# Sigmoid attention and two chained feed-forward layers in split float32: another order of the seven block products, and where the operands of the next pair are made

## The chip, the cores and the metric

The kernel runs on one core of a Trainium2 chip. The metric is the device time of one execution in microseconds (us), the median of several runs. Engines: PE (TensorE) multiplies, with PEld as its weight loads; DVE (VectorE), ACT (ScalarE) and POOL (GpSimd) work elementwise; SP (SyncE) issues nearly all DMAs. Each engine works through its own queue in order.

## The reference

```python
def _attn_ref(q, k, v):                      # 4 batches, 12 heads, 448 rows, 64 wide
    scores = (1 / np.sqrt(64)) * q @ k.transpose(0, 1, 3, 2) - np.log(448)
    return 1 / (1 + np.exp(-scores)) @ v

x = attention output as (1792, 768)
h = x @ moe_w_in                             # layer one: 768 -> 2048 -> 768
x = np.maximum(h, 0) ** 2 @ moe_w_out
h = x @ moe2_w_in                            # layer two, the same sizes
out = (np.maximum(h, 0) + alpha * np.minimum(h, 0)) @ moe2_w_out
```

Inputs q, k, v are float32; the weights and alpha come as float64.

## The kernel before

**Split operands.** A float32 operand of a product is kept as two float32r tiles, a high part (a cast by ACT) and the rest (a subtraction by DVE or POOL), and each product is three matmuls: high by high, high by rest, rest by high.

**Stages.** Attention comes first, twelve rounds `d` (L307), two blocks of two heads in each. Then 32 units (L510), numbered here 0 to 31: layer one with batches 0 and 1 ("pair" 0) is units 0 to 7, layer one with pair 1 units 8 to 15, layer two with pair 0 units 16 to 23, with pair 1 units 24 to 31. A unit takes 256 of the 2048 hidden columns, in two blocks `j` of 128, for the 896 tokens of its pair, in two halves `t` of 448.

**A unit.** First come seven block products of the Strassen-Winograd scheme instead of eight (`product(k)` L375, 9 matmuls each, into three PSUM banks `hb`). After each, `after(n, k)` (L403) adds the result to the running sums e21, e12, e22, e11 and, where one of the four hidden blocks is complete, `slopes` (L382) applies the layer's function and makes its high part, and `low` (L399) its rest, in `G`. In layer one `slopes` is three ACT instructions; in layer two it is two Relus on ACT, one DVE instruction that joins them with `nal` (alpha, negated), and an ACT cast. Then `out_products` (L448) multiplies `G` by the split output weights `WO`: 12 outputs of 448 columns in layer one, 14 of 384 in layer two, 6 matmuls each. Five PSUM banks `ob` take turns; the first four outputs begin with block j = 1 (two high matmuls each, then one of the rest each), and j = 0 follows. `collect` (L470) adds each bank to `acc` by one DVE instruction, or by an ACT copy in the first unit of a pair.

**Other work of a unit.** It is hung on the steps "i0" to "i6" (after each block product) and "o0" to "o13" (after each output) by `at` (L521). `out_parts` splits the output weights of this unit: ACT casts, POOL subtracts. For the next unit `weight_sum` makes four sums of blocks of its input weights on POOL, and `weight_parts` splits the seven blocks, 384 columns at a time (ACT, DVE). Weights are read once as float64 (`load` L82, two buffers `raw`), turned into float32 by two ACT instructions (`scale`) and a DVE one (`join`), and kept in DRAM; the second pair of each layer reads the kept words. So `scale` and `join` run in units 0 to 6 and 14 to 22.

**Change of pair.** The block products need seven split operands `X[0]` to `X[6]` of the pair's tokens. They are made (`x_jobs` L146: four sums and seven splits, three instructions of 448 columns for each sum and six for each split) for pair 0 of layer one in attention's last rounds and in unit 0, and for the other pairs within units 7, 15 and 23, the last units before each change of pair (L515 and L565 to L576).

## Time and profile before

| | us |
|---|---|
| median of 3 runs | 1239.09 (1238.93 to 1240.93) |
| the profiled execution | 1239.76 |
| its span, first to last instruction | 1238.0 |
| PE busy | 1111.8 (90%) |
| DVE busy | 766.4 (62%) |
| ACT busy | 624.7 (50%) |
| POOL busy | 422.3 (34%) |
| mean granted TensorE clock | 0.945 of full |

Busy time is that of the whole span. The stages differ: a stretch of the span is read from the windows, a wait from the timeline or from the list of waits, and the share of an engine over the whole span says nothing of one stage. The granted clock is the share of the 2.4 GHz clock that PE was given; it has two levels here, 1.0 and 0.5.

### The profile page before, as it was taken

The numbers are of one execution on the slowest core, as the hardware profiler recorded it, in microseconds if no ns is written. First come the engines' busy times: TensorE is split into PE (matmuls) and PEld (weight loads), VectorE is DVE, ScalarE is ACT, GpSimd is POOL, SyncE is SP. The second block draws the span as 40 slices with busy tenths as digits, with TensorE's granted clock in tenths as the row PEclk, the third lists the DMA queues.
The fourth block names the chain that finished last, engine by engine and source line by source line (L and its number), as shares of the span: only waits on it lengthen the run. The fifth ranks groups of instructions, "written<-read, shape, count | busy, mean of one in ns | idle before, by whom it ended". The sixth has DMA issues, their size and how long they took to land.

```text
span 1238.0 us, 14888 instructions
## 1 busy us (share of the span) xinstructions
PE 1111.8 (90%) x5607; PEld 953.7 (77%) x5607; DVE 766.4 (62%) x1121; ACT 624.7 (50%) x1055; POOL 422.3 (34%) x312
## 2 busy tenths in 40 slices
PE   6999989999998899999977888888896888898888
PEld 4555558888887788899966877888885777888877
DVE  3556854667777735565578467666678445555554
ACT  3567757666664464433455655555444543223332
POOL 0002352444344533333365223333343333332221
PEclk8999998999999999999989888888998989998899
DMA  5577703544442111111224433433422211111002
GB/s 119 122 184 194 199 1 130 177 153 153 154 153 89 38 52 64 52 65 51 77 77 153 152 116 115 138 109 136 154 77 73 93 52 41 50 39 51 26 26 90
DMA packets 108008, 123.67 MB, mean 100 GB/s; under 512 B 54048, under 2 KB 86560, under 8 KB 107936
## 3 DMA queue, kind: packets, MB, share of 16 engines
q1 hardware_dynamic: 105440, 121.47, 31.7%
q10 hardware_dynamic: 2496, 1.25, 0.4%
q8 instruction: 44, 0.72, 0.2%
q14 instruction: 28, 0.23, 0.1%
HBM read 92.02 MB, written 30.67 MB: 99 GB/s over the span
## 4 chain that ended last, share of the span: by engine, by line
PE 61%; DVE 18%; ACT 14%; issue 3%; DMA 2%; SPq 0%; POOL 0%; ACTq 0%; POOLq 0%; DVEq 0%
PE o L444 30%; PE h L380 19%; DVE c L396 5%; PE av L264 4%; PE sc L244 4%; DVE wi L139 3%; ACT pos L394 3%; ACT c L395 3%; DVE x L158 2%; DVE g L401 2%; ACT g L397 1%; ACT g L388 1%; ACT c L387 1%; ACT c L389 1%; ACT wi L138 1%
## 5 line engine op out<-in xcount | busy, mean ns | idle before, releaser
L380 PE MATMUL h<-x,wi 128*128 128x448 f32 x2016 | 426.1, 370 | 14.7 <-DVE c L415 10.9
L380 PEld LDWEIGHTS h<-x,wi 128*128 128x128 f32 x2016 | 380.3, 189 | 54.6 <-DVE c L415 8.2
L444 PE MATMUL o<-wo,g 128*128 128x384 f32 x1344 | 282.8, 372 | 74.8 <-DVE g L401 64.6
L444 PEld LDWEIGHTS o<-wo,g 128*128 128x128 f32 x1344 | 265.8, 213 | 91.9 <-DVE g L401 76.4
L530 POOL TENSOR_TENSOR wo<-wo,wo 128x768 fp32r<-128x768 f32 x64 | 129.6, 2045 | 451.2 <-ACT wo L529 451.2
L444 PE MATMUL o<-g,wo 128*128 128x448 f32 x1152 | 253.7, 378 | 22.7 <-DVE g L401 12.9
L444 PEld LDWEIGHTS o<-g,wo 128*128 128x128 f32 x1152 | 221.1, 194 | 53.1 <-DVE g L401 21.9
L481 DVE TENSOR_TENSOR acc<-o,acc 128x384 f32<-128x384 f32 (+1 forms) x364 | 208.1, 582 | 81.1 <-PE o L444 80.7
L139 DVE TENSOR_TENSOR wi<-wi,wi 128x384 fp32r<-128x384 f32 x96 | 95.9, 999 | 67.6 <-ACT wi L138 67.6
L401 POOL TENSOR_TENSOR g<-c,g 128x448 fp32r<-128x448 f32 x64 | 77.2, 1206 | 154.7 <-ACT g L397 103.2
L407 ACT ACTIVATE c<-h 128x448 f32<-128x448 f32 x32 | 17.3, 542 | 184.1 <-PE h L380 184.1
L396 DVE SCALAR_TENSOR_TENSOR c<-c,nal,pos 128x448 f32<-128x448 f32 x64 | 59.7, 933 | 72.0 <-ACT c L395 72.0
L246 ACT ACTIVATE a<-sc,bias 128x896 f32<-128x896 f32 x72 | 69.4, 1006 | 35.9 <-PE av L264 22.6
L139 DVE TENSOR_TENSOR wi<-s,wi 128x384 fp32r<-128x384 f32 x128 | 74.1, 579 | 13.5 <-ACT wi L138 13.4
L409 DVE TENSOR_TENSOR c<-h,c 128x448 f32<-128x448 f32 x32 | 20.0, 624 | 100.3 <-PE h L380 60.9
L158 POOL TENSOR_TENSOR x<-acc,x 128x448 fp32r<-128x448 f32 x32 | 44.8, 1406 | 102.6 <-ACT x L157 102.6
L127 POOL TENSOR_TENSOR s<-wi 128x384 f32<-128x384 f32 x32 | 40.5, 1267 | 89.6 <-DVE wi L113 89.6
L397 ACT ACTIVATE g<-c 128x448 fp32r<-128x448 f32 x64 | 37.0, 578 | 65.4 <-DVE c L396 65.4
L138 ACT ACTIVATE wi<-s 128x384 fp32r<-128x384 f32 x128 | 60.7, 513 | 0.0
L157 ACT ACTIVATE x<-acc 128x448 fp32r<-128x448 f32 x84 | 42.9, 565 | 33.2 <-DVE acc L152 31.4
L264 PE MATMUL av<-a,v 128*64 128x448 f32 x288 | 59.4, 548 | 0.0
L158 DVE TENSOR_TENSOR x<-acc,x 128x448 fp32r<-128x448 f32 x52 | 50.2, 999 | 12.3 <-ACT x L157 12.2
(164 smaller groups left out, 1116.0 us busy)
## 6 DMA issues: line engine op xcount, KB each, us to landing
v<-in_v_dram SPq DMA_DIRECT2D x24, 192.0 KB, 2.9
nat<-in_q_dram SPq DMA_DIRECT2D x22, 192.0 KB, 3.8
nat<-in_k_dram SPq DMA_DIRECT2D x20, 192.0 KB, 3.4
out_dram<-acc SPq DMA_DIRECT2D x14, 192.0 KB, 2.7
raw0i<-in_moe_w_in_dram SPq DMA_DIRECT2D x2, 768.0 KB, 5.8
raw0o<-in_moe_w_out_dram SPq DMA_DIRECT2D x2, 768.0 KB, 6.5
raw1i<-in_moe_w_in_dram SPq DMA_DIRECT2D x2, 768.0 KB, 5.3
raw1o<-in_moe_w_out_dram SPq DMA_DIRECT2D x2, 768.0 KB, 5.9
```

Source lines behind the costliest of these rows:

```text
L138: nc.scalar.activation(W[i][:, 0], w, AF.Copy)
L139: (eng or nc.vector).tensor_sub(W[i][:, 1], w, W[i][:, 0])
L158: jobs.append(lambda c=c: eng().tensor_sub(X[i][:, 1, c], x[c], X[i][:, 0, c]))
L244: nc.tensor.matmul(ps[:, h, :S], kt[rows, at:at + P], qt[rows, :S], start=(i == 0), stop=(i == 2))
L246: nc.scalar.activation(sig[u, j], ps[:, :, :S], AF.Sigmoid, bias=bias[:, :1], scale=SCALE)
L264: nc.tensor.matmul(avs[u][h * D:(h + 1) * D, :S], vals[u][:, h, j, :], a[:, h, :], start=(u % 2 == 0 and j == 0), stop=(u % 2 == 1 and j = ...
L380: nc.tensor.matmul(ps, W[k][:, wp, c * P:(c + 1) * P], X[k][:, xp, c], start=(k < 3 and c == 0 and i == 0), stop=(c == KH - 1 and i == 2), ...
L396: nc.vector.scalar_tensor_tensor(out=e, in0=e, scalar=nal[:, f:f + 1], in1=up, op0=ALU.mult, op1=ALU.add)
L401: eng.tensor_sub(gl, e, gh)
L444: nc.tensor.matmul(ps, *ops, start=(begin and i == 0), stop=(end and i == len(ways) - 1), skip_group_check=True)
L481: nc.vector.tensor_add(part, ps, part)
L530: nc.gpsimd.tensor_sub(WO[j][:, 1], words["o"][:, j], WO[j][:, 0])
```

## The change

- **Order of the block products.** `BANK` is now (0, 1, 2, 1, 2, 0, 1), and the hidden blocks come complete in the order e22, e12, e11, e21, one after each of products 3 to 6, where before it was e11, e22, e12, e21. The second part of a block (in layer two the DVE instruction and the cast) and its rest are issued one and two products later (`hidden`, `second`, `low`). All rests are made on DVE.
- **Input weights.** One tile `W` for all blocks; `weight_parts` splits 768 columns at a time in four pieces (s12 at i4, a1 at o0, a2 with 384 at o2, s34 at o3); the four sums run on DVE (i2, i3). The rests of the output weights stay on POOL, in four halves (i2 to i5).
- **Two banks at once.** `two` holds two PSUM tiles of two banks; a pair of outputs is added by one DVE instruction (768 or 896 columns). Seven of the eight banks are in use.
- **Words.** `turn_of`: scaling and joining now run in units 0 to 14, all in layer one; the words of layer two are joined in units 7 to 14 and go from `raw` straight to DRAM. `recall` reads kept words from unit 6 on.
- **X operands of the next pair.** X[0] to X[3] are made in units 1 to 6 of the pair before (four jobs a unit at o2 to o5: POOL sums and rests, ACT casts), through one tile `stage`, and sent to DRAM; the last unit of a pair loads them (i0 to i3) and makes X[4] to X[6] (DVE, DVE, POOL). Pair 1 of attention's output goes to DRAM (`late`) and comes back in unit 0. In attention all splits but X[6] are made, two subtractions of three on DVE (before one of three).

```diff
-        BANK = (0, 1, 2, 0, 1, 2, 1)
+        two = [psum.tile([P, 2, 512], F32, name="o0")]
...
+        BANK = (0, 1, 2, 1, 2, 0, 1)
+        OPERAND = (0, 4, 3, 5, 6, 1, 2)
...
+            for ways in (HIGH, LOW):
+                for os, both in pairs[:2]:
+                    for i in range(2):
+                        out_product(n, os[i], both[:, i], 1, ways, ways is HIGH, False)
+            for at, (os, both) in enumerate(pairs):
...
+                collect(n, os, both)
+                yield at
...
+        def wait_in_dram(p, i, c):
+            x_parts(p, i, c, nc.gpsimd, (stage[:, 0], stage[:, 1]))
+            nc.sync.dma_start(out=x_kept[i][:, :, c], in_=stage.bitcast(F32))
...
+            if V is not None:
+                if N > 1:
+                    at("i0", lambda: join(V, "i", 0))
+                    at("i1", lambda: join(V, "i", 1))
+                at("i0", lambda: load(V, "o", 0))
+                at("i1", lambda: load(V, "o", 1))
+                at("i5", lambda: scale(V, "o", 0, 1), lambda: scale(V, "o", 0, 0))
+                at("i6", lambda: join(V, "o", 0))
+                at("o0", lambda: scale(V, "o", 1, 1))
+                at("o1", lambda: scale(V, "o", 1, 0), lambda: join(V, "o", 1))
+            if U is not None:
+                at("i6", lambda: load(U, "i", 0))
+                at("o1", lambda: load(U, "i", 1))
+                at("o3", lambda: scale(U, "i", 0, 1), lambda: scale(U, "i", 0, 0))
+                at("o4", lambda: scale(U, "i", 1, 1))
+                at("o5", lambda: scale(U, "i", 1, 0))
...
+            step(3)
+            add(e22, 1, e22)
+            second22, low22 = hidden(n, e22, e22, 1, 1)
+            do("i3")
+            step(4)
+            add(e12, 2, e12)
+            second22()
+            second12, low12 = hidden(n, e12, e12, 0, 1)
+            do("i4")
+            step(5)
+            low22()
+            second12()
+            second11, low11 = hidden(n, hb[0][:, :S], e11, 0, 0)
+            do("i5")
+            step(6)
+            add(e21, 1, e21)
+            low12()
+            second11()
+            second21, low21 = hidden(n, e21, e21, 1, 0)
+            do("i6")
+            for i in out_products(n):
+                if i == 0:
+                    low11()
+                    second21()
+                if i == 1:
+                    low21()
+                do(f"o{i}")
```

DVE's queue from the middle of a layer-two unit into its outputs, before (c12 and so on are the sums e12 and so on, g0 and g1 the two tiles of `G`, o0 to o4 the output banks, wi the split input weights):

```order
L139 TENSOR_TENSOR wi3_79<-wi_87,wi3_79 128x384
L419 TENSOR_TENSOR c12_1765<-h2_1773,c12_1765 128x448
L396 SCALAR_TENSOR_TENSOR c12_1765<-c12_1765,nal_69,pos0_1767 128x448
L401 TENSOR_TENSOR g1_1762<-c22_1764,g1_1762 128x448
L423 TENSOR_TENSOR c21_1763<-h1_1772,c21_1763 128x448
L396 SCALAR_TENSOR_TENSOR c21_1763<-c21_1763,nal_69,pos1_1768 128x448
L401 TENSOR_TENSOR g0_1761<-c12_1765,g0_1761 128x448
L481 TENSOR_TENSOR acc1_75<-o4_1776,acc1_75 128x384
L139 TENSOR_TENSOR wi6_82<-wi_87,wi6_82 128x384
L481 TENSOR_TENSOR acc1_75<-o0_1769,acc1_75 128x384
L139 TENSOR_TENSOR wi1_77<-s2_84,wi1_77 128x384
```

and now (o0 and o1 are the tiles of two banks):

```order
L415 SCALAR_TENSOR_TENSOR c22_1787<-c22_1787,nal_69,pos0_1790 128x448
L137 TENSOR_TENSOR wi_77<-sums_78,wi_77 128x768
L417 TENSOR_TENSOR g1_1795<-c22_1787,g1_1795 128x448
L415 SCALAR_TENSOR_TENSOR c12_1788<-c12_1788,nal_69,pos1_1791 128x448
L582 TENSOR_TENSOR c21_1786<-h1_1800,c21_1786 128x448
L417 TENSOR_TENSOR g0_1794<-c12_1788,g0_1794 128x448
L415 SCALAR_TENSOR_TENSOR c11_1789<-c11_1789,nal_69,pos0_1790 128x448
L469 TENSOR_TENSOR acc1_1796<-o1_1802,acc1_1796 128x768
L417 TENSOR_TENSOR g0_1794<-c11_1789,g0_1794 128x448
L415 SCALAR_TENSOR_TENSOR c21_1786<-c21_1786,nal_69,pos1_1791 128x448
L137 TENSOR_TENSOR wi_77<-words_i_79,wi_77 128x768
L469 TENSOR_TENSOR acc1_1796<-o0_1798,acc1_1796 128x768
```

The split of s12 (`wi_77<-sums_78`) now stands ahead of the rest of e22, and between the first output's addition and the second's stand a rest, a layer-two join and the split of a1.

ACT's queue from the end of unit 9 (layer one, pair 1) into unit 10, before (L407 is the copy of the first product of unit 10):

```order
L389 ACTIVATE c21_1763<-c21_1763 128x448
L138 ACTIVATE wi6_82<-wi_87 128x384
L138 ACTIVATE wi1_77<-s2_84 128x384
L138 ACTIVATE wi2_78<-s1_83 128x384
L138 ACTIVATE wi4_80<-s3_85 128x384
L138 ACTIVATE wi5_81<-s4_86 128x384
L407 ACTIVATE c21_1763<-h0_1771 128x448
L529 ACTIVATE wo1_1760<-wo_88 128x768
L529 ACTIVATE wo0_1759<-wo_88 128x768
```

and now (raw words of layer two, `stage` the next pair's operands, L588 the copy of unit 10's first product):

```order
L136 ACTIVATE wi_77<-words_i_79 128x384
L158 ACTIVATE stage_1797<-acc0_76 128x448
L94 ACTIVATE raw19i0_3885<-raw19i0_3885 128x768
L96 ACTIVATE raw19i0_3885<-raw19i0_3885 128x768
L136 ACTIVATE wi_77<-sums_78 128x768
L158 ACTIVATE stage_1797<-acc0_76 128x448
L94 ACTIVATE raw19i1_3922<-raw19i1_3922 128x768
L158 ACTIVATE stage_1797<-acc0_76 128x448
L96 ACTIVATE raw19i1_3922<-raw19i1_3922 128x768
L588 ACTIVATE c21_1786<-h0_1799 128x448
L495 ACTIVATE wo1_1793<-words_o_80 128x768
```

Ahead of the copy stand now two casts into `stage` and the two scalings of a raw tile.

SP's queue from the end of unit 8 through unit 9, before (words of layer one that were kept):

```order
L88 DMA wi_87<-kept2i0_2027 128x768
L88 DMA wi_87<-kept2i1_2044 128x768
L88 DMA wo_88<-kept2o0_2158 128x768
L88 DMA wo_88<-kept2o1_2183 128x768
L88 DMA wi_87<-kept3i0_2246 128x768
L88 DMA wi_87<-kept3i1_2263 128x768
```

and now, from the middle of unit 9 into unit 10:

```order
L105 DMA kept18o0_3883<-raw18o0_3788 128x768
L86 DMA raw19i0_3885<-in_moe2_w_in_dram 128x6x128
L105 DMA kept18o1_3920<-raw18o1_3803 128x768
L86 DMA raw19i1_3922<-in_moe2_w_in_dram 128x6x128
L505 DMA kept_x8_0_3556<-stage_1797 256x1x448
L111 DMA words_i_79<-kept3i0_2249 128x768
L111 DMA words_i_79<-kept3i1_2264 128x768
L505 DMA kept_x8_0_3556<-stage_1797 256x1x448 x2
L105 DMA kept19i0_4009<-raw19i0_3885 128x768
L88 DMA raw19o0_4011<-in_moe2_w_out_dram 128x768
L105 DMA kept19i1_4024<-raw19i1_3922 128x768
```

Each load into `raw` stands behind the sending away of the words that lie in that buffer.

## Rows read from the trace of the kernel before

**Rows 1.** windows: us, busy us (count) by engine, PEclk, DMA share, GB/s
```profile
0.00:168.40 168.40, 157.74 (x1095) 86.84 (x1095) 95.19 (x117) 100.79 (x118) 22.45 (x22) 0.97 0.61 151
168.40:206.50 38.10, 31.33 (x137) 27.53 (x136) 23.13 (x27) 23.70 (x45) 18.34 (x13) 0.91 0.11 36
206.50:379.70 173.20, 169.09 (x812) 151.04 (x812) 121.55 (x179) 109.97 (x182) 70.22 (x49) 1.00 0.48 163
379.70:422.30 42.60, 32.70 (x136) 27.32 (x135) 34.42 (x45) 22.02 (x43) 23.67 (x18) 0.88 0.15 50
422.30:618.40 196.10, 194.74 (x947) 176.94 (x947) 106.71 (x174) 91.04 (x170) 74.16 (x58) 1.00 0.19 61
618.40:664.90 46.50, 34.09 (x136) 28.74 (x135) 39.64 (x50) 26.06 (x49) 25.01 (x18) 0.89 0.29 92
664.90:910.40 245.50, 215.57 (x1031) 200.36 (x1030) 161.14 (x241) 132.34 (x223) 83.56 (x58) 0.90 0.40 134
910.40:957.60 47.20, 34.09 (x148) 30.28 (x147) 37.79 (x53) 21.87 (x43) 25.03 (x18) 0.86 0.18 51
957.60:1204.00 246.40, 214.13 (x1031) 198.52 (x1030) 131.79 (x212) 88.17 (x168) 73.94 (x56) 0.92 0.15 50
```

**Rows 2.** timeline of PE in unit 28: start us, duration, instruction, count [idle before, releaser]
```profile
1098.17 13.17 PE L380 MATMUL h<-x,wi 128*128 128x448 f32 x63
1112.12 1.67 PE L444 MATMUL o<-wo,g 128*128 128x384 f32 x8 [0.78 <-ACT g L397]
1116.14 1.34 PE L444 MATMUL o<-wo,g 128*128 128x384 f32 x6 [2.34 <-DVE g L401]
1119.14 15.04 PE L444 MATMUL o<-wo,g 128*128 128x384 f32 x69 [1.67 <-DVE g L401]
```

**Rows 3.** timeline of DVE in unit 28
```profile
1112.99 0.62 DVE L419 TENSOR_TENSOR c<-h,c 128x448 f32<-128x448 f32 x1
1114.86 0.69 DVE L396 SCALAR_TENSOR_TENSOR c<-c,nal,pos 128x448 f32<-128x448 f32 x1 [1.25 <-ACT c L395]
1115.46 0.62 DVE L401 TENSOR_TENSOR g<-c,g 128x448 fp32r<-128x448 f32 x1
...
1119.87 0.56 DVE L481 TENSOR_TENSOR acc<-o,acc 128x384 f32<-128x384 f32 x1 [0.78 <-PE o L444]
1120.34 0.55 DVE L139 TENSOR_TENSOR wi<-wi,wi 128x384 fp32r<-128x384 f32 x1
```

**Rows 4.** timeline of ACT in unit 28
```profile
1115.58 0.58 ACT L397 ACTIVATE g<-c 128x448 fp32r<-128x448 f32 x1 [0.75 <-DVE c L396]
```

**Rows 5.** windows: a stretch of unit 28, and unit 31 with the final stores
```profile
1118.40:1125.20 6.80, 6.05 (x19) 6.06 (x20) 5.12 (x12) 2.64 (x6) 1.15 (x1) 0.50 0.20 59
1204.00:1238.00 34.00, 28.32 (x148) 26.17 (x147) 15.01 (x26) 8.73 (x15) 5.96 (x4) 1.00 0.26 82
```

**Rows 6.** timeline of PE in unit 31
```profile
1222.15 12.41 PE L444 MATMUL o<-wo,g 128*128 128x384 f32 x70 [1.68 <-DVE g L401]
```

**Rows 7.** groups by line: count, busy us, mean ns of one, idle before
```profile
L529 ACT ACTIVATE wo<-wo 128x768 fp32r<-128x768 f32 x64 | 50.4, 838 | 0.0
...
L158 POOL TENSOR_TENSOR x<-acc,x 128x448 fp32r<-128x448 f32 x32 | 44.8, 1406 | 102.6 <-ACT x L157 102.6
...
L217 DVE COPY flat<-tp 128x896 f32<-128x896 f32 x23 | 24.0, 1085 | 18.7 <-PE tp L214 18.7
```

**Rows 8.** DMA issues: count, KB each, median us from issue to landing
```profile
raw5i<-in_moe_w_in_dram SPq DMA_DIRECT2D x2, 768.0 KB, 5.4
...
kept5o<-wo SPq DMA_DIRECT2D x2, 384.0 KB, 3.4
```

**Rows 9.** timeline across the start of unit 4: PE and ACT
```profile
293.87 5.33 PE L380 MATMUL h<-x,wi 128*128 128x448 f32 x25
...
296.14 0.91 ACT L103 ACTIVATE raw5i<-raw5i 128x768 f32<-128x768 f32 x1 [1.82 <-DMA raw5i<-in_moe_w_in_dram]
...
297.75 0.53 ACT L407 ACTIVATE c<-h 128x448 f32<-128x448 f32 x1
```

More of the change, by code (lines that the diff above doesn't have):

```diff
@@ L107, in join @@
     def join(n, kind, j):
-        if (n, kind, j) not in raws:
-            return
         raw = raws.pop((n, kind, j))
-        to = words[kind][:, j]
-        nc.vector.scalar_tensor_tensor(out=to.bitcast(I32), in0=raw[:, :, 1], scalar=3, in1=raw[:, :, 0], op0=ALU.logical_shift_left, op1=ALU.bitwise_or)
-        _, f = source(n, kind, j)
-        keep = kept[UNITS[n][0], f, kind] = dpool.tile([P, DM], F32, name=f"kept{n}{kind}{j}")
-        nc.sync.dma_start(out=keep, in_=to)
-    def block(i, half):
-        return words["i"][:, i, half * HALF:(half + 1) * HALF]
@@ L121, in weight_sum @@
-    def weight_sum(i):
-        s1, s2, s3, s4 = sums
-        a11, a12, a21, a22 = block(0, 0), block(0, 1), block(1, 0), block(1, 1)
-        nc_ = nc.gpsimd
+        layer, p, fp = UNITS[n]
+        to = words[kind][:, j].bitcast(I32) if layer == 0 else raw.rearrange("p m t -> p (m t)")[:, :DM]
+        nc.vector.scalar_tensor_tensor(out=to, in0=raw[:, :, 1], scalar=3, in1=raw[:, :, 0], op0=ALU.logical_shift_left, op1=ALU.bitwise_or)
+        keep = kept[layer, 2 * fp + j, kind] = dpool.tile([P, DM], F32, name=f"kept{n}{kind}{j}")
@@ new lines, in join, with recall, turn_of, weight_sum @@
+        nc.sync.dma_start(out=keep, in_=to.bitcast(F32))
+    def recall(n, kind):
+        layer, p, fp = UNITS[n]
+        for j in range(2):
+            nc.sync.dma_start(out=words[kind][:, j], in_=kept[layer, 2 * fp + j, kind])
+    def turn_of(n):
+        return n if n < NB else n + NB
+    def weight_sum(i, eng=None):
+        (a11, a12), (a21, a22) = ([words["i"][:, j, h * HALF:(h + 1) * HALF] for h in range(2)] for j in range(2))
+        s = [sums[:, k * HALF:(k + 1) * HALF] for k in range(4)]
+        eng = eng or nc.vector
@@ L299, in fused_kernel @@
             early = [(0, "i", 0), (0, "i", 1), (0, "o", 0), (0, "o", 1), (1, "i", 0), (1, "i", 1)]
[L300 removed]
+            turns = [0]
             def either():
[L303 to L306 removed]
+                turns[0] += 1
+                return nc.gpsimd if turns[0] % 3 == 0 else nc.vector
+            ready_x = []
+            for what in X_ORDER[:-1]:
+                make = x_sums if what[0] == "s" else x_parts
+                ready_x += [lambda i=int(what[1]), c=c, make=make: make(0, i, c, either()) for c in range(KH)]
             for d in range(ND):
@@ L581, in fused_kernel @@
-            for i in range(7):
-                product(i)
-                after(n, i)
-                do(f"i{i}")
-                if i == 6:
-                    low(e21, 1, 0, nc.gpsimd)
-            for i in out_products(n):
+            if n == 0:
+                at("i0", lambda: nc.sync.dma_start(out=acc[1], in_=late))
+                for c in range(KH):
+                    at(f"i{c}", lambda c=c: x_parts(0, 6, c, nc.vector))
+            at("i0", lambda: out_parts(1), lambda: out_parts(0))
@@ new lines, in add, with step @@
+            def add(to, bank, other):
+                nc.vector.tensor_add(to, hb[bank][:, :S], other)
+            def step(k):
+                product(k)
+            step(0)
+            nc.scalar.activation(e21, hb[0][:, :S], AF.Copy)
+            do("i0")
+            step(1)
+            add(e12, 1, e21)
+            do("i1")
+            step(2)
+            add(e22, 2, e21)
+            do("i2")
+            step(3)
+            add(e22, 1, e22)
+            second22, low22 = hidden(n, e22, e22, 1, 1)
```

320 lines of the change are left out of this document (136 added, 184 removed).

## The prediction

> **What bounds the kernel now.** I read the windows by stage first, then the timelines of PE, DVE and ACT in single units, then the groups by line and the DMA issues. The windows [rows 1] show three regimes. Attention, the first 168.4 us, has PE busy for 157.7, and DVE for 95.2. Layer one's ordinary units (1 to 6, 8 to 14) are bound by PE at the full clock: 173.2 us for six units is 28.9 each, 196.1 for seven is 28.0. Layer two's (16 to 22, 24 to 30) take 245.5 and 246.4 us for seven, 35.1 and 35.2 each, at a granted clock of 0.90 and 0.92. The four units that make X operands, 0, 7, 15 and 23, take 38.1, 42.6, 46.5 and 47.2: there DVE is busy 23 to 40 us, POOL 18 to 25, and the clock is 0.86 to 0.91.
>
> Why layer two takes 7 us more than layer one, with as much to multiply, is seen in unit 28 [rows 2]: the seven products run through in 13.2 us, then PE waits 0.78, 2.34 and 1.67 us in the outputs, for the hidden blocks' parts. The 69 matmuls behind the last wait show 15.0 us, where 70 took 12.4 in unit 31, with a longest wait of 1.68 [rows 6]. The windows say why: unit 28 has 6.8 us at 0.50, half of 2.4 GHz, and unit 31 stays at 1.00 [rows 5]. So a layer-two unit is 13.0 + 84 x 0.177 = 27.9 us of work, 4.8 of waiting and 2 to 3.5 of half clock.
>
> DVE and ACT hand the blocks to and fro meanwhile [rows 3, 4]. The add of a product starts at 1112.99, the two Relus end 1.87 later, the join (0.69) and the rest (0.62) follow at 0.60 after each other, ACT's cast starts 0.04 after the join and takes 0.58.
>
> **The change, part by part.** Costs are against the profiled execution, 1239.8 us (1.8 of it outside the span of 1238.0); the median of the runs, 1239.1, is 0.7 lower.
>
> *Layer two's ordinary units, 13 of them (17 to 22, 25 to 30).* I walk DVE's new queue with T = 0 at the unit's first product. Product 4 can be added at 9.5 (five sevenths of 13.0, and 0.2). Add 0.55, join to 10.75, cast of e22 to 11.35, the Relus of e12 to 12.5. Then comes s12, 768 columns: ACT 0.84 [rows 7], to 13.3; DVE has no row of this size, two of 384 take 0.55 + 0.48 [rows 3], so 0.84 to 1.03, and I take 0.95: 14.25. Behind it in the same queue: the rest of e22, 14.8; join of e12, 15.45; its cast, 16.05; the Relus of e11, 17.0; its join, 17.7; cast and the Relus of e21, 19.5; its join, 20.2; cast, 20.8; then a1, 0.84 and 0.95, to 22.6; and only then the addition of the second pair of banks, 768 columns again, to 23.5. PE's side: outputs from 13.0, the eight high matmuls to 14.45, wait 0.4 for the rest of e22, 0.55 and 0.3 for e12's parts, the first two pairs done at 18.6, the first added by 18.75, third pair to 20.9. The fourth needs the second tile: it waits to 23.5, **2.6 us**. Four pairs of 12 x 0.177 follow: 32.1. That is 4.2 us of waiting against 4.8. Its longest wait is above the 2.34 that went with a half clock in unit 28 and above the 1.68 that did not in unit 31 [rows 2, 5, 6], so I keep the half clock at the price of [rows 1]: a clock of 0.92 over 246.4 us is 19.7 us for seven units, 2.8 each. 34.9 against 35.1: **-3** for 13 units. With the first units of the two pairs, 16 and 24, whose outputs ACT copies (-2), and unit 31, which has no s12 and no a1 (-2): **-7**.
>
> The double addition itself: one of 384 takes 0.56 and the next starts 0.48 later [rows 3], so two in one save some 0.1 us of DVE and release the first bank 0.4 later. DVE is busy 131.8 of 246.4 us in layer two's second half [rows 1], far from full, so I count the saving at nothing and the late release within the waits above. The Trainium skill (Perfetto Trace Analysis, Optimizing Scalar/DVE Operations) says that grouping pays where an engine is saturated, and that an engine which is not, but leaves bubbles in others, is better served by smaller instructions. By that rule splits of 384 and banks one by one would give back most of the 2.6 us; by counting instructions alone, ten wide ones a unit at 0.1 would be 32 us gained over the 32 units. The trace stands with the rule.
>
> *The X operands.* In units 1 to 6 of a pair, four jobs stand at o2 to o5: POOL 1.41 us each [rows 7], under outputs where POOL had been idle or made sums; ACT casts of 0.58 as in [rows 4]. Through one tile `stage` each cast waits for the last one's DMA: 1.4 + about 3.4 (kept words of 384 KB, a little smaller, take that [rows 8]), 5 us against 2.2 to 2.5 between steps, so ACT ends such a unit late, the cover of its next casts being the 2.1 us until the next unit's first product. What is left in units 7, 15 and 23: three splits of three column blocks, on ACT 9 casts, on DVE 6 rests. Walked like the above, the rest of X[4] stands ahead of e12's rest, X[5]'s between the additions: unit 7 about 34 and a half clock, 36.6 (**-6**); unit 15, without words now, 32.5 (**-14**); unit 23, with the joins of layer two between, 43 (**-4**). Their bounds: 28.0 and 35.1 each, as if all were hidden (-15, -18, -12), and nothing gained.
>
> *Unit 0.* 24 X instructions leave; six come (X[6]), and ACT's copies stay: 32.6 for 38.1, **-5.5** (bounds 0 and -9, the 28.9 of its neighbours).
>
> *Attention.* Two subtractions of three on DVE in place of one make 20 where 6 were, 14 more at 0.62 (as the rests in [rows 3]): 8.7 us on an engine busy 95 of 168 [rows 1], in its later rounds more. Bounds 0 and +8.7; I take **+2**, nearer to nothing since PE had work throughout.
>
> *Layer one, first half (1 to 6).* Waits by the same walk: 0.4 for the first pair's addition and 0.75 for the second's (behind a join of words and a1; 896 columns at 1.085 [rows 7]): 29.2 for 28.9, **+2**.
>
> *Layer one, second half (8 to 14).* It now scales and joins words, which it did not. Each raw buffer must first be sent away: a join at T = 22.9, kept by 26.3 (3.4), loaded by 31.7 (5.4) [rows 8], 2.7 us into the next unit. ACT scales it (0.91 twice) ahead of the copy of product 0, which then comes at about 4.6. Unit 4 did the same before: ACT waited for a raw tile, and the copy came 3.9 us into the unit [rows 9], whose like took 28.9. Here the copy moves product 3 by 0.2 to 1 and all behind it by 1.5, in units with three casts through `stage` more: 30.9 on average for units 9 to 13, 29.5 for unit 14, 32 for unit 8, whose outputs ACT copies. 216 for 196 (with 28.0 at best): **+19**, bounds 0 and +35.
>
> Sum: -7 - 6 - 14 - 4 - 5.5 + 2 + 2 + 19 = -13.5. 1239.1 - 13.5 is **1225.5 us**, faster by 1.1%.
>
> **The rivals.** *The clock stays up in layer two.* The waits are spread over 9 us where they stood within 7, and layer two's second half, at 0.92, already loses less to the clock than the first, at 0.90 [rows 1]. Without the half clock, 13 x 2.8 = 36 us more are gained: 1189. For it: unit 31, with no wait above 1.68, stayed at 1.00 [rows 5, 6]. Against it: a single wait of 2.6 is longer than any in unit 28. *The words of layer two come too late (slower).* If a keep and a load take 2 us more between them, in a layer one that now moves words, operands and kept words at once, product 0's copy comes at 6.6, product 3 waits 2 us, and the clock falls: 2 + 2.8 in the six units 8 to 13 is 29 us: 1254. It decides from a raw tile that lands 4 us or more into its unit. For it: DMA share was 0.48 in units 1 to 6 with less to move [rows 1]. Against it: a copy at 3.9 did no harm. *Two tiles of banks make the clock oscillate in layer one too (slower).* There PE would stop briefly at two pairs in each unit; at 2.8 us in 14 units: 1225.5 + 39 = 1265. Against it: units 1 to 6 show 1.00 with 4.1 us of PE idle among them [rows 1]. The Trainium skill (TensorE: Matmul & The Clock Gate, A second HAM failure mode) tells of a kernel in which cycling through PSUM banks made short pauses and the clock swung; this trace shows no such swing at short pauses, so the chance is small. *The bursts are only moved*, with the time within 0.2%: what units 7, 15, 23 and 0 save (29.5) layer one pays again.
>
> **How the numbers follow.** Forecast 0.51 (1208 to 1236), clock up 0.18, late words 0.19, clock in layer one 0.05, bursts only moved 0.07. Differences under 0.2%, 2.5 us, can't be told from none here. Faster: 0.51 + 0.18 = 0.69; same 0.07; slower 0.24. The range leaves out a tenth on either side: the clock-up case reaches down to 1186, late words up to 1257.
>
> **What would show it.** Right: in an ordinary layer-two unit a PE wait of 2 to 3 us ahead of the fourth pair, released by DVE's two-bank addition, and a half clock behind it; units 7, 15 and 23 at 32 to 43 us; units 8 to 14 at 29.5 to 32, with ACT waiting for raw tiles. Wrong: layer-two units under 33 or over 36.5 us, layer one's second half still at 28 or above 34, attention over 175.

## The result, and the profile after

The changed kernel takes 1227.03 us (median of 4 runs, 1223.79 to 1228.03) where the kernel before takes 1239.51 (1238.93 to 1240.93): a ratio of 0.9893, interval 0.9872 to 0.9914. The forecast of 1225.5 is off by 1.5 us. Its terms are much further off, by some 30 us in places, on both sides, and cancel. Two single executions, 2078.73 us of the kernel before and 3624.61 of run 8, lie far above all others and are in no ratio; without it the median of run 8 is 1226.79.

The windows of the changed kernel, cut at the same places of the program as [rows 1] (attention, unit 0, units 1 to 6, 7, 8 to 14, 15, 16 to 22, 23, 24 to 30, 31 with the last stores), with the same columns:

```profile
0.00:158.60 158.60, 155.89 (x1096) 85.13 (x1096) 104.16 (x128) 103.03 (x121) 19.15 (x20) 1.00 0.65 166
158.60:188.70 30.10, 28.02 (x138) 25.33 (x137) 16.95 (x24) 21.50 (x34) 4.71 (x4) 1.00 0.65 230
188.70:386.40 197.70, 176.83 (x811) 153.87 (x810) 137.06 (x161) 113.37 (x175) 63.04 (x48) 0.97 0.53 170
386.40:420.30 33.90, 29.00 (x137) 24.99 (x136) 22.84 (x31) 18.28 (x30) 4.98 (x4) 1.00 0.82 304
420.30:665.50 245.20, 210.11 (x946) 184.09 (x945) 155.68 (x185) 137.45 (x211) 72.22 (x55) 0.94 0.61 207
665.50:697.50 32.00, 28.69 (x137) 25.02 (x137) 21.55 (x29) 15.52 (x28) 8.37 (x7) 1.00 0.57 222
697.50:928.20 230.70, 210.08 (x1031) 190.75 (x1030) 140.00 (x189) 89.11 (x152) 59.84 (x52) 0.96 0.21 72
928.20:966.90 38.70, 31.87 (x148) 29.05 (x147) 24.13 (x34) 15.24 (x28) 8.57 (x7) 0.91 0.63 217
966.90:1192.10 225.20, 207.07 (x1031) 188.06 (x1030) 134.22 (x189) 82.83 (x140) 29.96 (x28) 0.98 0.16 53
1192.10:1224.50 32.40, 28.06 (x148) 26.21 (x147) 15.50 (x21) 8.44 (x15) 3.93 (x4) 0.98 0.27 86
```

Set against [rows 1] and [rows 5] (spans, 1238.0 and 1224.5 us):

| stretch | before | after | difference | the prediction's term |
|---|---|---|---|---|
| attention | 168.4 | 158.6 | -9.8 | +2 |
| unit 0 | 38.1 | 30.1 | -8.0 | -5.5 |
| units 1 to 6 | 173.2 | 197.7 | +24.5 | +2 |
| unit 7 | 42.6 | 33.9 | -8.7 | -6 |
| units 8 to 14 | 196.1 | 245.2 | +49.1 | +19 |
| unit 15 | 46.5 | 32.0 | -14.5 | -14 |
| unit 23 | 47.2 | 38.7 | -8.5 | -4 |
| layer two, the rest | 525.9 | 488.3 | -37.6 | -7 |
| sum | 1238.0 | 1224.5 | -13.5 | -13.5 |

Three places hold the errors; each was then tried on the chip.

**Attention's start.** The kernel before has a gap there that the prediction never looked at. Its PE, DVE and SP timelines, one row or two each:

```profile
17.32 0.74 PE L244 MATMUL sc<-qkh 64*128 64x448 f32 x2 [8.27 <-DVE qkh L221]
```
```profile
16.10 0.17 DVE L288 TENSOR_SCALAR nal<-al 128x16 f32<-128x16 f32 x1 [14.76 <-DMA al<-in_moe_alpha_dram]
16.18 1.08 DVE L221 CAST qkh<-tp 128x896 fp32r<-128x896 f32 x1
```
```profile
12.73 0.60 SPq L287 DMA_DIRECT2D al<-in_moe_alpha_dram  x1
```

DVE stands 14.8 us at the negation of alpha, whose DMA SP issues behind 16 others; the queries' cast behind it in DVE's queue has long had its input. PE idles 8.27 us, and its first two matmuls behind that take 0.74 us, for 0.47 in the changed kernel, where PE goes on:

```profile
8.97 0.47 PE L245 MATMUL sc<-qkh 64*128 64x448 f32 x2
```

The full diff moves that one line, which the core shown above leaves out and the prediction passed over:

```diff
-            nc.vector.tensor_scalar(out=nal, in0=al, scalar1=-1.0, scalar2=None, op0=ALU.mult)
...
+                if d == 2:
+                    nc.vector.tensor_scalar(out=nal, in0=al, scalar1=-1.0, scalar2=None, op0=ALU.mult)
```

**Layer one.** The groups by line of the DMAs out of `stage` (L505), and who waited for them:

```profile
L505 SPq DMA_DIRECT2D kept_x<-stage x36: 512/519/622, 214.3 to 918.3; - x36
...
  ACT stage L158: 84.8, 18
...
DMA to landing us min/median/max: 2.9/2.9/7.2
```

In the whole kernel ACT stood 84.8 us, 18 times, for that tile. The timelines of ACT, SP and PE from unit 1 (starts at 188.7) into unit 2 (218.4) show what it does:

```profile
209.25 0.56 ACT L158 ACTIVATE stage<-acc 128x448 fp32r<-128x448 f32 x1
...
221.04 0.58 ACT L158 ACTIVATE stage<-acc 128x448 fp32r<-128x448 f32 x1 [6.87 <-DMA kept_x<-stage]
...
225.87 0.58 ACT L158 ACTIVATE stage<-acc 128x448 fp32r<-128x448 f32 x1 [3.45 <-DMA kept_x<-stage]
...
227.14 0.52 ACT L588 ACTIVATE c<-h 128x448 f32<-128x448 f32 x1
```
```profile
212.40 0.33 SPq L105 DMA_DIRECT2D kept2o<-words_o  x1
212.82 1.39 SPq L86 DMA_DIRECT2D raw3i<-in_moe_w_in_dram  x1
214.31 9.12 SPq L505 DMA_DIRECT2D kept_x<-stage  x2
```
```profile
228.37 4.10 PE L396 MATMUL h<-x,wi 128*128 128x448 f32 x10 [4.32 <-DVE c L582]
```

The first cast's DMA is issued at 214.31, 5 us after the cast: SP stands until 212.40 at the sending of joined words, whose join DVE ends only then, and then issues a load of raw words. It also lands late, behind that load of 768 KB; this is the time to landing of the one DMA issued between 214 and 222:

```profile
DMA to landing us min/median/max: 6.7/6.7/6.7
```

The second cast waits till 221.04, the third 4.8 us more, and the copy of unit 2's first product comes 8.7 us into the unit. DVE adds behind it, and PE waits 4.32 us for a bank ahead of the fourth product (the prediction's product 3; the expectations below call it product 4). So, more or less, in units 2, 3, 5, 6, 10, 11, 13 and 14 (33.4 to 37.7 us each, 283 together); units 4, 9 and 12 take 30.4 to 30.9. Unit 8 waits 7.24. Behind the waits of 3.4 us and more PE shows a half clock too. An estimate from the windows, the missing share of the clock times the stretch, is 6 us in units 1 to 6 (0.97) and 15 in units 8 to 14 (0.94).

**Layer two.** PE, then DVE in unit 26 (1030.65 to 1062.32):

```profile
1046.61 5.04 PE L434 MATMUL o<-wo,g 128*128 128x384 f32 x24 [0.24 <-ACT g L416]
1053.90 8.58 PE L434 MATMUL o<-wo,g 128*128 128x384 f32 x48 [2.25 <-DVE acc L469]
```
```profile
1049.86 0.68 DVE L415 SCALAR_TENSOR_TENSOR c<-c,nal,pos 128x448 f32<-128x448 f32 x1
1051.92 0.96 DVE L137 TENSOR_TENSOR wi<-words_i,wi 128x768 fp32r<-128x768 f32 x1 [1.38 <-ACT wi L136]
1052.80 0.95 DVE L469 TENSOR_TENSOR acc<-o,acc 128x768 f32<-128x768 f32 x1
```

This is the wait the prediction walked out: 2.25 us for 2.6, the addition at 22.2 us into the unit for 22.6. Its other waits are 0.18 and 0.24 for 1.25 together. But unit 26 takes 31.7 us and shows no half clock; units 25 and 27 with the same waits show 0.95 and take 33.2.

### The profile page after: what moved, and what is told of

The parts are those of the page before. It is cut to its first block, busy times and chain, and to the rows that moved or that the text cites. A ratio compares the mean times of both kernels' runs of the same rounds, so it can differ in the third digit from the quotient of the medians.

```text
span 1224.5 us, 14729 instructions
## 1 busy us (share of the span) xinstructions
PE 1105.6 (90%) x5607; PEld 932.5 (76%) x5607; DVE 772.1 (63%) x990; ACT 604.8 (49%) x933; POOL 274.8 (22%) x229
## 3 DMA queue, kind: packets, MB, share of 16 engines
q10 hardware_dynamic: 2496, 1.25, 0.4%
## 4 chain that ended last, share of the span: by engine, by line
PE 37%; DVE 25%; ACT 19%; DMA 12%; issue 5%; POOL 1%; SPq 1%; ACTq 0%; DVEq 0%
PE o L434 17%; PE h L396 11%; DMA kept_x<-stage 4%; ACT wi L136 4%; PE av L265 3%; DVE c L582 3%; DVE c L415 3%; PE sc L245 3%; DVE sums L125 3%; DVE acc L469 3%; DVE wi L137 2%; ACT g L416 2%; DVE g L417 2%; ACT g L404 2%; ACT c L412 2%
## 5 line engine op out<-in xcount | busy, mean ns | idle before, releaser
L396 PE MATMUL h<-x,wi 128*128 128x448 f32 x2016 | 435.9, 377 | 34.1 <-DVE c L582 34.1
L499 POOL TENSOR_TENSOR wo<-words_o,wo 128x384 fp32r<-128x384 f32 x128 | 152.7, 1226 | 354.9 <-ACT wo L495 354.7
L469 DVE TENSOR_TENSOR acc<-o,acc 128x768 f32<-128x768 f32 (+1 forms) x182 | 184.5, 1015 | 73.3 <-PE o L434 72.0
L582 DVE TENSOR_TENSOR c<-h,c 128x448 f32<-128x448 f32 x160 | 98.9, 618 | 144.4 <-PE h L396 83.2
L137 DVE TENSOR_TENSOR wi<-sums,wi 128x768 fp32r<-128x768 f32 x64 | 61.2, 957 | 109.5 <-ACT wi L136 109.5
L159 POOL TENSOR_TENSOR stage<-acc,stage 128x448 fp32r<-128x448 f32 x36 | 41.2, 1145 | 363.0 <-ACT stage L158 363.0
L417 DVE TENSOR_TENSOR g<-c,g 128x448 fp32r<-128x448 f32 x128 | 88.7, 693 | 3.6 <-ACT g L416 1.9
L588 ACT ACTIVATE c<-h 128x448 f32<-128x448 f32 x32 | 17.2, 538 | 148.5 <-PE h L396 137.8
L247 ACT ACTIVATE a<-sc,bias 128x896 f32<-128x896 f32 x72 | 69.1, 1005 | 35.6 <-PE av L265 22.6
L137 DVE TENSOR_TENSOR wi<-words_i,wi 128x768 fp32r<-128x768 f32 x64 | 48.4, 757 | 40.2 <-ACT wi L136 40.2
L403 ACT ACTIVATE c<-c 128x448 f32<-128x448 f32 x48 | 27.5, 573 | 73.8 <-DVE c L582 73.8
L158 ACT ACTIVATE stage<-acc 128x448 fp32r<-128x448 f32 x36 | 20.5, 571 | 84.8 <-DMA kept_x<-stage 84.8
L151 POOL TENSOR_TENSOR acc<-acc 128x448 f32<-128x448 f32 x40 | 57.3, 1450 | 0.1
L136 ACT ACTIVATE wi<-sums 128x768 fp32r<-128x768 f32 x64 | 53.0, 829 | 0.0
```

The source lines that it names most:

```text
L136: nc.scalar.activation(hi, w, AF.Copy)
L137: nc.vector.tensor_sub(lo, w, hi)
L151: eng.tensor_sub(to[c], x[c], y[c])
L247: nc.scalar.activation(sig[u, j], ps[:, :, :S], AF.Sigmoid, bias=bias[:, :1], scale=SCALE)
L396: nc.tensor.matmul(ps, W[:, wp, at:at + P], X[k][:, xp, c], start=(k < 3 and c == 0 and i == 0), stop=(c == KH - 1 and i == 2), skip_group ...
L417: return second, lambda: nc.vector.tensor_sub(gl, e, gh)
```

## The experiments

Medians are compared with 1227.03 for the changed kernel, ratios with the kernel before.

**1. Alpha back in front (alpha_first).** The diff above, undone.

> The changed kernel with one line put back to where it stood before: DVE's negation of alpha stands again ahead of attention's first round, instead of in its third round. Theory A: in the kernel before, DVE waited there for the DMA that brings alpha, which SP issues only at 12.7 us behind 16 others; PE had its gap of 8.27 us at 9 us and half clock behind it. Then the first scores start again at about 17 us instead of 9.0, attention ends at 168 instead of 158.6, and the time is 1227 + 9.8 = 1237 us (1235 to 1238). Rival: attention became shorter for another reason (pair 1's output sent away, no copies of X[6], the order of the early weight loads); then the gap does not come back, or PE makes it up, and the time stays at 1227.

Measured: 1237.45 us (ratio 0.9987, 0.9975 to 0.9998). PE's gap is back:

```profile
17.65 0.74 PE L245 MATMUL sc<-qkh 64*128 64x448 f32 x2 [8.66 <-DVE qkh L222]
```

**2. The kernel before with that line moved alone (before_alpha_third).**

> The kernel before with that one line alone moved as the change moves it (the negation of alpha in attention's third round). Theory A: the gap of 8.27 us and the half clock behind it go, all else stays: 1239.5 - 9.8 = 1229.7 us (1228 to 1232), so that all the rest of the change together is worth some 3 us. Rival: the gap is only moved to another place of attention (the queries of the later rounds wait for the same loads): 1237 to 1240.

Measured: 1228.85 us, where the kernel before took 1238.72 on the same chip (0.9915, 0.9895 to 0.9935); attention ends at 157.9, the other units are as before:

```profile
0.00:157.90 157.90, 155.92 (x1096) 86.12 (x1096) 95.14 (x117) 100.61 (x118) 22.45 (x22) 1.00 0.65 161
```

Theory A stands from both sides. Nearly the whole gain of the change is one line; all the rest comes to some 2 us, in which large gains and losses cancel.

**3. A second tile for the operands on their way (stage_two_tiles).**

```diff
-            x_parts(p, i, c, nc.gpsimd, (stage[:, 0], stage[:, 1]))
+            turns["x"] += 1
+            way = both_pos.bitcast(F32R) if turns["x"] % 2 and turns["x"] <= 8 * KH else stage
+            x_parts(p, i, c, nc.gpsimd, (way[:, 0], way[:, 1]))
...
```

> The changed kernel with a second tile for the operands on their way to DRAM in layer one (the two tiles that only layer two uses take turns with stage; layer two keeps the one). Theory S: in layer one ACT waits for the DMA that empties stage, so the copy of a unit's first product comes 8 to 9 us into units 2, 3, 5, 6, 10, 11, 13 and 14; these eight take 283.2 us, and would take about 30.5 each as units 4 and 9 do, 244. Expected 1227 - 30 = 1197 us (1190 to 1205), with PE's waits ahead of product 4 under 1 us in all units but 8. Rival W: the raw words of layer two come too late, and the stage only stands beside it; then units 2, 3, 5, 6 come down to 30.5 (-15) but 10, 11, 13, 14 stay over 34: 1212. Rival Q: the DMAs wait in SP's queue behind a load, and a second tile helps by half: units of three casts still wait 2 us, 1210.

Measured: 1192.99 us (0.9627, 0.9611 to 0.9643), 34 less than the change, 30 of them in units 1 to 14. Units 1 to 6 and 9 to 14:

```profile
188.60:372.10 183.50, 171.42 (x811) 150.09 (x811) 136.12 (x161) 113.26 (x175) 66.18 (x48) 1.00 0.57 183
444.90:635.90 191.00, 174.13 (x812) 150.78 (x811) 136.29 (x161) 111.83 (x173) 64.53 (x48) 0.99 0.66 224
```

No unit but 8 waits ahead of the fourth product any more; the eight units take 252.7 us. Theory S holds, and W falls as a cause by itself, but for unit 8, which waits 8.62 us. The other 4 us or so are in layer two, where fewer units show a half clock; the edit does not touch it (see the end of the document).

**4. The same DMA issued by POOL (stage_pool_queue).**

```diff
-            nc.sync.dma_start(out=x_kept[i][:, :, c], in_=stage.bitcast(F32))
+            nc.gpsimd.dma_start(out=x_kept[i][:, :, c], in_=stage.bitcast(F32))
```

> The changed kernel with one word changed: the DMA that empties stage is issued by POOL, which has just made the rest, and no longer by SP. Theory Q: in SP's queue it stands behind a load that waits for its raw buffer; the first cast of a unit at o2 is followed by its DMA only 2.3 to 5.1 us after POOL's subtraction, so the cycle of one tile is 7 to 12 us there against 4.8 where the DMA is issued at once. Issued at once, the three casts of a unit come at 21.5, 26.3 and 31.1 us, and the copy of the next first product at 2 to 4 us: no wait ahead of product 4 but in unit 8, 1227 - 30 = 1197 us (1190 to 1205). Rival S (one tile, whatever the queue): the third cast still holds ACT and half the wait stays: 1212. A rival on the other side: issuing from POOL takes so long there that the sums and the rests of the output weights come late: 1227 or more.

Measured: 1250.98 us (1.0094, 1.0079 to 1.0109), slower than both kernels. At first theory Q is right for ACT: unit 1's casts are at 209.87, 216.91 and 222.10, and the copy comes 4.3 us into unit 2, not 8.7. Yet PE waits 6.71 us there, ahead of the fifth product, and the copies of later units come late again (9.6 us into unit 3). POOL and DVE in unit 2:

```profile
224.22 0.68 POOL L505 DMA_DIRECT2D kept_x<-stage  x1 [0.30 <-POOL stage L159]
224.83 1.26 POOL L151 TENSOR_TENSOR acc<-acc 128x448 f32<-128x448 f32 x1
225.94 3.94 POOL L499 TENSOR_TENSOR wo<-words_o,wo 128x384 fp32r<-128x384 f32 x4
229.76 2.28 POOL L151 TENSOR_TENSOR acc<-acc 128x448 f32<-128x448 f32 x2
```
```profile
224.49 8.38 DVE L103 SCALAR_TENSOR_TENSOR words_i<-raw3i 128x768 int32<-128x768 int32 x1
232.79 0.61 DVE L582 TENSOR_TENSOR c<-h,c 128x448 f32<-128x448 f32 x1
```

A join of 0.95 us lasts 8.38, until 0.8 us after POOL's seven instructions behind its DMA issue are done, and the addition that frees PE's bank stands behind it. This is not what the expectation's rival said (POOL late): DVE is held. See run 11. So this run tells what the DMA costs in POOL's queue, and does not settle how much of the change's wait is SP's queue.

**5. The jobs by column block (stage_by_column).**

```diff
+                    waiting = [waiting[k * KH + c] for c in range(KH) for k in range(len(X_WAITING))]
```

> The changed kernel with the 24 operand jobs of a pair in another order: all eight jobs of one column block first (split, sum, split, sum and so on), then the next block, so that every unit has exactly two casts into stage, at o2 and o4, with a sum on POOL between, where it had three, two or one. Theory S with Q: a cast at 21.5 us, its DMA behind SP's loads, the second cast free at 30 to 33 us, that is up to 4 us into the next unit, and the copy of the first product at 6 at most, which is early enough for product 4. Expected: PE's waits ahead of product 4 under 1 us in units 2 to 7 and 9 to 15, 1227 - 30 = 1197 us (1190 to 1207). Rival: each unit then waits a little, 1 to 2 us, in place of every second one 4: 1227 - 15 = 1212.

Measured: 1206.66 us (0.9724, 0.9702 to 0.9746). No wait ahead of the fourth product but 10.2 us in unit 8; the rival is partly right too, since each ordinary unit of layer one but 8 now waits 2 to 3.8 us among its outputs.

**6. a1 behind the second double addition (a1_after_add).**

```diff
-                at("o0", lambda: weight_parts("a1"))
+                at("o1", lambda: weight_parts("a1"))
```

> The changed kernel with the split of a1 (ACT cast and DVE rest of 768 columns) one step later, behind the second double addition. Theory: in a layer-two unit PE waits 2.25 us for that addition, which stands behind the rest of e11, the join of e21 and the rest of a1 (0.95 us) on DVE. With a1 behind it the wait is 1.3 us: 13 units x 0.95 = 12 us less, and if the half clock of 3.4 us, which follows in every second unit and costs 1.5, goes as well, 12 more: 1227 - 12 = 1215 (1202 to 1217). Rival: DVE is idle 1.4 us ahead of that rest, waiting for ACT's cast; the addition could stand there at once, so all 2.25 us less the end of the e21 join would go, 1227 - 24 - 12 = 1191. Rival on the other side: the rest of e21 now comes later, and the third and fourth outputs' wait is only moved to the next pair: 1227.

Measured: 1179.42 us (0.9516, 0.9485 to 0.9548), 48 less than the change and below every value expected. DVE and PE in its unit 26, and the windows of units 17 to 22 and 25 to 30:

```profile
1015.07 0.69 DVE L415 SCALAR_TENSOR_TENSOR c<-c,nal,pos 128x448 f32<-128x448 f32 x1
1015.67 0.95 DVE L469 TENSOR_TENSOR acc<-o,acc 128x768 f32<-128x768 f32 x1
```
```profile
1011.81 13.72 PE L434 MATMUL o<-wo,g 128*128 128x384 f32 x72 [0.24 <-ACT g L416]
```
```profile
716.60:898.20 181.60, 175.29 (x884) 156.86 (x883) 125.42 (x167) 73.30 (x127) 56.97 (x48) 1.00 0.25 83
966.30:1143.50 177.20, 174.28 (x883) 156.93 (x883) 118.80 (x167) 67.25 (x115) 25.97 (x24) 1.00 0.16 50
```

The addition now starts right behind the e21 join, the whole wait of 2.25 goes, not 0.95 of it (its first rival), and so does every half clock in these units: 29.5 us each (31.7 in units 18 and 21), and 358.8 for the twelve units that took 395.0 (and 420.8 before the change). What had stood ahead of the addition was not DVE's 0.96 us of work alone but also DVE's wait of 1.38 for ACT's cast of a1. Layer one's units 1 to 7 gained 11 more.

**7. Words of layer two joined in layer two (words_in_layer_two).**

```diff
-            V = turn_of(N) if N < 2 * NB else None
-            U = turn_of(M) if M < 2 * NB else None
+            V = N if N < NU and N // NB % 2 == 0 else None
+            U = M if M < NU and M // NB % 2 == 0 else None
...
```

> The changed kernel with the words of layer two scaled and joined in units 14 to 22, as before the change, and no longer in units 7 to 14. Theory W: in layer one's second half the keep of the last words, the load into the same buffer and two scalings stand ahead of each first product's copy, and unit 8 waits 7.2 us: units 8 to 14 come from 245.2 to the shape of units 1 to 6 (about 33 each, 230) or lower, layer two's first half stays at 231 as it did not suffer from the joins before the change: 1227 - 15 = 1212 (1205 to 1217). Rival S (the one stage tile alone holds ACT): units 10, 11, 13, 14 still wait 4 us, only unit 8 loses its wait, and layer two pays for the joins on DVE ahead of the hidden blocks: 1222 to 1235.

Measured: 1211.45 us (0.9772, 0.9742 to 0.9801), the time that W gave. Units 8 to 14 and 17 to 22:

```profile
419.10:619.40 200.30, 196.73 (x946) 177.35 (x945) 119.03 (x155) 94.27 (x155) 64.75 (x52) 0.99 0.26 87
685.60:914.00 228.40, 187.32 (x884) 167.68 (x883) 153.55 (x190) 109.20 (x174) 62.83 (x48) 0.94 0.45 145
```

The parts are larger than W's: layer one's second half gains 45 us, with one stage tile and yet no wait ahead of the fourth product, and layer two pays 28 in these six units. So, but for unit 8, neither the one tile nor the words are enough alone: ACT's copy is late where both are there. In unit 9 the first cast now comes at 18 us, not 21.8; its DMA is issued at once behind POOL's rest and lands in 3.2 us, where in the changed kernel it is issued 4.2 us later and lands in 6.3; and the third cast is done 2 us into the next unit. The run takes the scalings out of ACT's queue and the loads out of SP's together; what each is worth is not shown.

**8. The two banks added one by one (banks_one_by_one).**

```diff
-                nc.vector.tensor_add(part, both, part)
+                for e in range(2):
+                    nc.vector.tensor_add(part[:, e], both[:, e], part[:, e])
```

> The changed kernel with each pair of banks added by two DVE instructions of one bank each instead of one of two banks (the pairs of tiles and the order stay). Theory P (the place in the queue decides): in layer two the second pair's addition still stands behind the rest of a1, so PE's wait of 2.25 us shortens only by the half of the addition that the next output's first bank no longer needs, 0.4 us: 13 x 0.4 = 5 us less, and 0.1 us of DVE more for each pair, which nothing waits for: 1222 (1218 to 1229). By the rule of the Trainium skill (Perfetto Trace Analysis, Optimizing Scalar/DVE Operations), smaller instructions serve an engine that leaves bubbles in others: most of the 2.25 us would come back, 1227 - 20 = 1207. By counting DVE's time alone: 182 additions more at 0.1, 18 us slower.

Measured: 1227.43 us (0.9891, 0.9867 to 0.9916), as the change. PE's wait in its unit 26:

```profile
1055.73 8.56 PE L434 MATMUL o<-wo,g 128*128 128x384 f32 x48 [2.24 <-DVE acc L470]
```

P is right that the place decides; its own 0.4 us did not come. The rule of the Trainium skill (Perfetto Trace Analysis, Optimizing Scalar/DVE Operations) is that breaking up instructions may let work be done sooner where an engine that is not saturated leaves bubbles in others. By it the prediction expected most of the wait back; smaller additions in the same order left it as it was. The splits of 384 columns, which the prediction named with them, were not tried.

**9. Both edits together (both_moves).** Runs 3 and 6.

> The changed kernel with both edits that gained: the second tile for the operands on their way to DRAM in layer one, and the split of a1 behind the second double addition. If the two act in different places, the gains add: the second tile alone came to 1193.0, the later a1 takes 37.8 us out of layer two's units 17 to 30 (33.2 and 31.7 each became 29.5), and in layer one the wait ahead of the fourth pair, about 1 us in each of 14 units, goes too: 1193 - 38 - 10 = 1145 us (1138 to 1156). Rival: in layer one the units that run faster meet the raw words of layer two later (with a1 moved and one stage, units 12 to 14 wait 4.5 to 6.3 us ahead of product 4, where unit 12 had no wait before): then layer one's second half gives 15 us back, 1165 to 1175.

Measured: 1147.81 us (0.9266, 0.9241 to 0.9292), 79 less than the change: the gains add (34 + 48 = 82). Units 1 to 6 take 173.9 us, as before the change (173.2 in [rows 1]), though they now make and send the next pair's operands. They, unit 8, and units 9 to 14:

```profile
188.60:362.50 173.90, 168.33 (x812) 151.10 (x811) 130.49 (x161) 113.92 (x176) 66.76 (x48) 1.00 0.60 197
396.30:434.30 38.00, 30.27 (x137) 27.18 (x137) 19.47 (x25) 25.51 (x38) 8.89 (x7) 0.87 0.62 207
434.30:623.30 189.00, 172.10 (x811) 153.14 (x810) 131.55 (x161) 111.60 (x173) 65.06 (x48) 0.98 0.68 227
```

**10. The second raw tile scaled behind the copy (scale_behind_copy).** `scale(U, "i", 1, ...)` at o4 and o5 becomes `scale(V, "i", 1, ...)` at i0 of the next unit.

> The kernel of the run before (both moves) with the two scalings of the second raw tile of input weights behind the copy of the next unit's first product on ACT, instead of at o4 and o5 ahead of it. Theory: what is left of the late words is unit 8, where PE waits 8.6 us because the copy stands behind the scalings of a tile that lands 10.6 us into the unit; the copy comes some 4 us earlier there, and in units 10 to 14 no copy waits for a raw tile any longer: 5 to 12 us less than the run before. Rival on the other side: the join of that tile now stands on DVE at i1, between the additions of products 1 and 2, and waits there for the scalings: PE then waits ahead of product 4 or 5 in every unit of layer one, 13 x 1 us or more slower.

Measured: 1148.33 us (0.9265, 0.9239 to 0.9292), no difference. Both sides came true: unit 8 takes 34.6 us for 38.0 and units 9 to 14 185.9 for 189.0, but units 1 to 6 take 179.5 for 173.9, with PE waiting 0.3 to 0.9 us in five of them.

**11. A small DMA by POOL ahead of its rests (pool_dma_ahead).**

```diff
+            if n > NU - NB:
+                spare = dpool.tile([P, 16], F32, name=f"spare{n}")
+                at("i2", lambda spare=spare: nc.gpsimd.dma_start(out=spare, in_=WO[1][:, 0, :16].bitcast(F32)))
```

> The kernel with both moves, and in layer two's second half (units 25 to 31) one more small DMA a unit, of 16 columns into spare DRAM, issued by POOL right ahead of its four rests of the output weights. It measures what was seen where POOL issued the DMAs of stage: there a DVE instruction of two SBUF operands that met POOL's work behind such an issue took as long as that work lasted (8.4 us of a normal 0.95). Theory L: the issue is what does it; then POOL's four rests take 1.0 each, and DVE's first sum of input weights (0.55) lasts to their end, 1.5 to 2.5 us in each unit. Rival: it was the size or number of the DMAs in flight, or the sums of operands among POOL's work; then DVE's two sums take 0.55 and 1.25 as without the DMA, and the four rests 4.3. The time changes little either way: 1148 to 1160.

POOL and DVE in unit 28 without it (run 9), then with it:

```profile
1028.03 4.33 POOL L500 TENSOR_TENSOR wo<-words_o,wo 128x384 fp32r<-128x384 f32 x4 [25.18 <-ACT wo L496]
```
```profile
1030.93 0.55 DVE L123 TENSOR_TENSOR sums<-words_i 128x384 f32<-128x384 f32 x1
1031.52 1.25 DVE L125 TENSOR_TENSOR sums<-sums,words_i 128x384 f32<-128x384 f32 x1
```
```profile
1033.30 0.56 POOL L531 DMA_DIRECT2D spare<-wo  x1 [26.02 <-ACT wo L496]
1033.88 3.92 POOL L500 TENSOR_TENSOR wo<-words_o,wo 128x384 fp32r<-128x384 f32 x4
```
```profile
1035.99 2.23 DVE L123 TENSOR_TENSOR sums<-words_i 128x384 f32<-128x384 f32 x1
1038.26 0.56 DVE L125 TENSOR_TENSOR sums<-sums,words_i 128x384 f32<-128x384 f32 x1
```

Theory L holds: POOL's four rests end at 1037.80, and the sum, begun at 1035.99, only 0.4 us later; POOL is faster, 0.98 each for 1.08. So it is in all six units from 25 to 30 (2.23 to 2.37 us for the sum). There was one execution, 1156.37 us.

**12. Both edits and the jobs by column (both_by_column).**

> The kernel with both moves, and the operand jobs of a pair by column block too (two casts a unit, at o2 and o4). Theory: what is left of the stage in layer one is unit 12, which waits 4.2 us behind a unit with one cast, and the short waits of units 10, 13 and 14; with two casts in every unit and two tiles none waits: 5 to 8 us less than both moves alone, 1141. In layer two, which has the one tile, units 18 and 21 with three casts (31.7 us against 29.5) come down by 2 each: 1137 to 1143 in all. Rival on the other side: with the jobs by column POOL works beside DVE in every unit instead of in two of three, and DVE's sums and joins of two SBUF operands grow; the outputs of all units of layer one then wait 1 us more, as with one tile (2 to 3.8 us there): 1148 to 1160.

Measured: 1149.91 us (1142.81 to 1150.51; 0.9273, 0.9257 to 0.9289), no difference from run 9. In the profiled execution, the fastest, units 18 and 21 take 29.5 us for 31.7, as the theory had it, but unit 8 takes 40.2 for 38.0 and unit 10 34.1 for 32.1. Whether it is better stays open: the medians say not.

## Why the prediction came out right, and where it was wrong

The time, the range and the direction were right, the time by luck: errors of -12, -31 and +53 us, with smaller ones of -10 together, cancel. Two of the prediction's own signs of being wrong came: four ordinary units of layer two took 31.7 us, under its 33, and units 8 to 14 took 35.0 each on the mean, above its 34.

- **Attention, +2 (measured -9.8).** The step that failed: "nearer to nothing since PE had work throughout". [Rows 1] held the warning, 157.74 us busy of 168.4, a granted clock of 0.97 and 10.7 us of idle that the prediction did not place. Runs 1 and 2 put 9.9 to 10.4 us on one line. The 14 subtractions that it did price show (DVE 104.16 us busy for 95.19), and cost little: attention ends at 158.6 with them, and at 157.9 in run 2 without them.
- **Units 1 to 6, +2 (measured +24.5).** The tile was named: "5 us against 2.2 to 2.5 between steps, so ACT ends such a unit late". The step stops there: it was not carried on to the copy of the next first product, and its cover, given as 2.1 us, was run over by 6.6. A cycle takes 4.8 us (225.87 less 221.04) where SP issues at once, but 11.8 where the DMA goes out behind a load: it was issued 3.3 us after POOL's rest was done and landed 6.7 us later, for 2.9, and neither was in a term. With two tiles units 1 to 6 come back to 183.5, and with a1 moved as well to 173.9.
- **Units 8 to 14, +19 (measured +49).** The mechanism was priced by its likes, whose copy at 3.9 us did no harm [rows 9]; this held in units 9 and 12 (copies at 3.8 and 3.6), but in units 10, 11, 13 and 14 the copy came at 7.7 to 9.3. In its effect this is the rival of late words (its 2 us of wait are 3.4 to 4.9 there). Its sign, a raw tile that lands 4 us or more into its unit, came in unit 8 alone (9.0 us); in units 10 to 14 it landed at 1.6 to 2.0. There ACT waited for `stage`: in unit 10 the cast at 492.45 waits 6.16 us for it, and the scaling at 492.93 follows without a wait. The cause has two parts, the one tile and the words' share in the queues: run 3 takes one away, run 7 the other. Of the 49 us some 15 are half clock (the estimate above), which the prediction had in its rival alone.
- **Layer two, -7 (measured -37.6).** The walk of DVE's queue held within 0.4 us at its end (its 4.2 us of waiting in all is some 0.3 more than the waits that it lists). Two sizes failed: the earlier waits (1.25 us, measured 0.42) and the half clock, kept at 2.8 us in every unit because "Its longest wait is above the 2.34 that went with a half clock in unit 28". With longest waits of 2.2 to 2.3 us (1.6, twice, in unit 21) the half clock came in 8 of the 12 units and cost some 1.5 there; so the rival with the clock up came half true. The first units of the pairs, 16 and 24, put at -2, gained 10: 30.4 and 30.5 us for 36.4 and 34.7, at a full clock. And the ordinary units (17 to 22, 25 to 30) are twelve, not thirteen as the prediction counts.
- **Units 0, 7, 15 and 23, -29.5 (measured -39.7).** Right in kind; each is within 4.5 us of its term, and all four land within their bounds.
- **Double additions, nothing.** Right (run 8). The walk even holds why the second stood so late, a wait for ACT's cast of a1 (from 20.2 to 21.6 in it). What it did not ask is whether that split, which nothing needed yet, had to stand there; run 6 says no.
- **The clock oscillating in layer one**, a rival, was not seen: units there without a long wait stay at 1.00.

## What to carry to other kernels

In a queue that works in order, ask of every instruction ahead of a critical one what it waits for, not only how long it lasts: alpha's negation (0.17 us of work, 14.8 of waiting), the split of a1 (0.96 us, whose cast came late) and a cast into a tile that a DMA empties cost 10, 48 and 34 us here, and each was cured by one move or one more tile. Place all the idle time of the bounding engine in every stretch before pricing a change, the start of the program too. And walk a single-buffered tile through its whole cycle, with the queue that issues its DMA and what was issued just ahead of it: a transfer that lands in 2.9 us alone and in 6.7 behind a load made cycles of 4.8 and 11.8.
